# Gelu of an MLP taken one token tile at a time, between the exponentials of an attention that shares ScalarE with it

## The chip, the cores and the metric

The kernel runs on one core of one Trainium2 chip. The metric is the device time of one execution in microseconds (us), here the median of the runs. The core has five engines that each work through their own list of instructions in order: TensorE (PE in the profile, with PEld for the loading of weights), VectorE (DVE), ScalarE (ACT), GpSimd (POOL) and SyncE (SP), which here only issues DMAs. They wait for each other by semaphores.

## The reference

Two layers of the same kind follow each other on 2048 tokens of width 512. Each has an attention part with 32 query heads of width 16 that share one key and one value head, and a part B with a token-shifting mixer and an MLP. Cut to what matters:

```python
def _A_ref(x, wq, wk, wv, wo):              # S = 2048, D = 512, H = 32, Dh = 16
    q = (x @ wq).reshape(B, S, H, Dh).transpose(0, 2, 1, 3)
    k, v = x @ wk, x @ wv                   # one head for all queries
    p = _softmax(jnp.einsum("bhqd,bkd->bhqk", q, k) * (Dh ** -0.5))
    return jnp.einsum("bhqk,bkd->bhqd", p, v)....reshape(B, S, H * Dh) @ wo

def _B_ref(x, w1, w2, w3, w4):              # F = 1792
    h = _gelu(_layernorm(x) @ w1)           # tanh form of gelu
    ...                                     # the four quarters of h are shifted by +1, -1, +2, -2 tokens
    x1 = x + shifted @ w2
    return x1 + _gelu(_layernorm(x1) @ w3) @ w4

x = x + _A_ref(_layernorm(x), ...)
x = x + _B_ref(_layernorm(x), ...)          # and both once more, with the same weights
```

## The kernel before

The program is laid out by a list scheduler that runs while the kernel is built. Every operation is declared with the tags that it reads and writes, an estimated duration `dur` and a priority (a lower number goes first); the scheduler walks through an estimated time, gives each engine the ready operation with the lowest number, and so fixes the order of each engine's instructions and the semaphores between them. On the chip only that order and those waits remain: where the estimate was too early, an engine stands still; where it was too late, work is placed later than it could be.

Tokens come in 16 tiles of 128, grouped in chunks. Layer 0 has four chunks of four tiles; layer 1 has three of four and two of two tiles:

```python
CHUNKS = (((0, 4), (4, 4), (8, 4), (12, 4)),
          ((0, 4), (4, 4), (8, 4), (12, 2), (14, 2)))
EARLY = (6, 11)      # layer 1, chunk 0: key tiles 0-5 first, then 6-10, then 11-15
SPILLED = 7          # for so many blocks of four heads; their sums are spilled in between
```

The attention of a chunk is cut into blocks of four heads, and these into halves: two heads, 512 queries and 128 keys (two key tiles and 256 queries in short chunks), that is 128x1024 scores. The whole program has 2048 halves. A half goes one of two ways. As a *unit*, ScalarE takes the exponential of both heads at once from PSUM:

```python
def declare_unit(self, g):
    ...
    q = op("PE", fpe, reads=self.inputs(g), writes=bk, ...)            # scores = K^T Q into PSUM
    o = op("ACT", lambda e: e.activation(self.EA[:, ea, :, :], self.PB[:, b0:b0 + 2, :], ACTF.Exp, scale=0.25),
           writes=bk + [("EA", ea)], dur=0.06 + 1024 / 1200, prio=0, ...)
    self.add_pv(g, ...)                                                # times V, summed in the PSUM bank ACC
```

As a *pair*, VectorE and GpSimd take it: VectorE scales the scores to 16-bit integers that are read as bf16 (J), one instruction per head; GpSimd, or VectorE if GpSimd has a queue, makes two shifted copies (JK); and the three are multiplied with three scaled copies of V, which averages the error of the piecewise-linear exponential:

```python
def assign(self, now, p):                    # may the next half be a pair?
    ...                                      # x pairs at most may be unfinished
    if self.pl.backlog() > y or self.waiting and ...:
        return False
    ...
    self.declare_pair(g)
```

When a block's sum is complete, VectorE copies it out of ACC, which frees ACC for the next block; ACCF, RZ and OS, the buffers of the steps that follow, are each two deep:

```python
def block_end(self, la, c, b, end):
    m = self.nfin % 2
    acc, rz = self.ACCF[:, m, 0:n], self.RZ[:, m, 0:4 * nq]            # n = 512, or 256 in short chunks
    self.last_copy = op("DVE", lambda e: e.tensor_copy(acc, self.PB[:, self.ACC, 0:n]), writes=[("AC",), ("ACCF", m)], ...)
    ...                                      # row sums, reciprocal, spread by TensorE
    op("DVE", ... self.OS[:, m, 0:n] = acc * spread ..., reads=[("ACCF", m)], writes=[M, ("OS", m)])
    ...                                      # OS goes to OT by DMA, or by TensorE in the last blocks
```

When all eight blocks of a chunk are done, `chunk_end` declares its output projection, mixer and MLP, which run beside the attention of later chunks. The MLP lags by one tile, because the mixer needs tokens of the next chunk: it runs for tiles 0-2, 3-6, 7-10 and, in layer 0, 11-13 and 14-15.

```python
def chunk_end(self, la, c):
    ...
    if m < 0:
        self.qproj(la, c + 2, prio=11)       # Q of the chunk after next, staged in QS and moved to QT by DMA
    self.mixer_in(la, c, tiles, tail, ...)
    ...
    for p in ([grp] if len(grp) <= 4 else [grp[:3], grp[3:]]):
        self.mlp(la, p, tail, self.DEFER[la][c])
    self.next_kv(la, c)                      # layer 0: K and V of layer 1 for the finished tiles

def mixer_in(...):
    ...                                      # x W1 on TensorE, copied to GP by VectorE
    op("ACT", fg, reads=gt + ..., writes=gt + ..., dur=2.7 + 4 * n / 1200 + ..., prio=-1)   # gelu of GP in place

def mlp(self, la, tiles, tail, defer=False):
    ...                                      # layer norm, transposes
    for f in range(14):
        ...                                  # 128 of the 1792 features: W3 on TensorE (128x32 pieces, four side by side)
        op("DVE", ... self.G2[:, f, 0:n] <- PSUM ..., writes=[L, ("G2", f)])
    g2 = [("G2", f) for f in range(14)]
    def fgelu(e):
        for a in (0, 7):                     # two instructions, seven feature blocks of all tiles each
            ins = e.activation(self.G2[:, a:a + 7, 0:n], self.G2[:, a:a + 7, 0:n], ACTF.Gelu_apprx_tanh)
        return ins
    if not tail:
        op("ACT", fgelu, reads=g2, writes=g2, dur=2.8 + 14 * n / 1200, prio=-1)
    self.mlp_out(la, tiles, tail)            # per tile: 56 products with W4, then the residual added by VectorE
```

The exponential and the gelu need different activation tables, so that the program holds a table load ahead of each change from one to the other. Where TensorE would have nothing to do for long, the scheduler puts in filler products of zeros (`ONES,NIL`), which keep it active.

Of the kernel before, what the change touches and what calls it, by code (L numbers as in the profile page):

```python
# [26 lines left out]
class Op:  # L27
    __slots__ = ("eng", "emit", "preds", "npend", "succ", "dur", "prio", "seq", "ready", "start",
                 "end", "take", "give", "dma", "out", "pos", "sem", "vc", "side", "placed", "pe", "feeds", "port", "parts")


class Plan:
# [65 lines left out]
    def op(self, eng, emit, reads=(), writes=(), dur=0.1, prio=None, take=None, give=None,  # L98
           dma=0, out=False, side=True, pe=None, port=False, parts=1):
# [5 lines left out]
        o.parts = parts  # L105
        o.feeds = None
# [204 lines left out]

    def backlog(self):
        return sum(o.dur for o in self.heap["DVE"] if o.side and o.ready <= self.now + 0.5)

    def _place(self, o, t):
# [31 lines left out]
        else:  # L347
# [5 lines left out]
            o.end = t + wait + o.dur + self.DRAIN[o.eng]  # L353
# [152 lines left out]
class Kernel:  # L506
# [20 lines left out]
    DEFER = ((False, False, False, False, False), (False, False, False, False, False))  # L527
# [11 lines left out]
    SOON = 0.45  # L539

# [23 lines left out]
    def memory(self):  # L564
# [24 lines left out]
        self.OS = sb("OS", [2, 512])  # L589
# [11 lines left out]
        self.ACCF = sb("ACCF", [2, 512])  # L601
        self.RZ = sb("RZ", [2, 16])
# [57 lines left out]
    def head(self):  # L660
# [70 lines left out]
        self.qproj(0, 1)  # L731
# [72 lines left out]
    def ln_in(self, la, tiles, prio=None):  # L804
# [6 lines left out]
        base = (self.QS, "QS") if la else (self.ZR, "ZR")  # L811
# [54 lines left out]
    def qproj(self, la, c, prio=None, blocks=range(8), direct=False):  # L866
        op = self.pl.op
        tiles = self.tiles_of(la, c)
# [5 lines left out]
        for k in () if direct else range(blocks[0] // 2, blocks[-1] // 2 + 1):  # L874
            L = Late()
            for h in range(2):
# [7 lines left out]
            op("DVE", lambda e, k=k, L=L: e.tensor_copy(self.QS[:, k, 0:n], self.PB[:, L.bank, 0:n]),  # L884
               writes=[L, ("QS", k)], dur=t_ps(n), prio=prio, give=L)
        if not direct:
            k0, k1 = blocks[0] // 2, blocks[-1] // 2 + 1
            for j in range(2):
                op("SP", lambda e, j=j: [
                    e.dma_start(self.QT[32 * h:32 * h + 16, par, 2 * k0 + j:2 * k1:2, 0:n],  # L890
                                self.QS[64 * j + 16 * h:64 * j + 16 * h + 16, k0:k1, 0:n]) for h in range(4)],
                   reads=[("QS", k) for k in range(k0, k1)], writes=[("QT", par, 2 * k + j) for k in range(k0, k1)],
# [20 lines left out]
    def make_groups(self):  # L913
# [49 lines left out]
        self.later = None  # L963
# [141 lines left out]
    def block_end(self, la, c, b, end):  # L1105
# [12 lines left out]
        m = self.nfin % 2  # L1118
        self.nfin += 1
        n = self.size(la, c)  # L1120
        nq = n // 128
        acc, rz = self.ACCF[:, m, 0:n], self.RZ[:, m, 0:4 * nq]
        if end == "add":
# [3 lines left out]
               reads=tags, writes=[("AC",), ("ACCF", m)], dur=t_ps(512), prio=0, side=False)  # L1127
        else:
            self.last_copy = op("DVE", lambda e: e.tensor_copy(acc, self.PB[:, self.ACC, 0:n]),  # L1129
               writes=[("AC",), ("ACCF", m)], dur=t_ps(n), prio=0, side=False)  # L1130
# [9 lines left out]
        op("PE", fz, reads=[("ACCF", m), ("SELC",)], writes=[L], pe=("F", 60 * nq, 4 * nq), prio=fin, take=L)  # L1140
# [4 lines left out]
        op("DVE", frec, writes=[L, ("RZ", m)], dur=0.17, prio=fin, give=L)  # L1145
        M = Late()
        for h in range(nq // 2):
# [8 lines left out]
            op("PE", fx, reads=[("RZ", m), ("ID",)], writes=[M], pe=("P", 256, 256, range(4)), prio=fin,  # L1156
               take=M if h == 0 else None)
        op("DVE", lambda e: e.tensor_tensor(out=self.OS[:, m, 0:n], in0=acc, in1=self.PB[:, M.bank, 0:n],  # L1158
                                            op=ALU.mult),
           reads=[("ACCF", m)], writes=[M, ("OS", m)], dur=t_ps(n), prio=fin, give=M)  # L1160
        r0 = 64 * (b % 2)
        hw = n // 2
        if c == len(self.CHUNKS[la]) - 1 and b >= self.LATE_OT:
            N = Late()

            def fo(e):
                ins = None
                for u in range(2):
                    for p in range(2):
                        x = r0 + 32 * p  # L1170
                        ins = e.matmul(self.PB[x:x + 32, N.bank, u * hw:u * hw + hw], lhsT=self.SELO[:, u, :],
                                       rhs=self.OS[:, m, p * hw:p * hw + hw], start=True, stop=True,
                                       tile_position=(0, x), skip_group_check=True)
                return ins
            op("PE", fo, reads=[("OS", m)] + [("SELO", i, u) for i in range(2) for u in range(2)], writes=[N],
# [3 lines left out]
        else:  # L1179
            op("SP", lambda e: [  # L1180
                e.dma_start(self.OT[r0 + 16 * (2 * p + i):r0 + 16 * (2 * p + i) + 16, b // 2, u * hw:u * hw + hw],
                            self.OS[32 * (2 * i + u):32 * (2 * i + u) + 16, m, p * hw:p * hw + hw])
                for p in range(2) for i in range(2) for u in range(2)],
               reads=[("OS", m)], writes=[("OT", b)], dma=128 * n, parts=8, prio=fin)
# [40 lines left out]
    def assign(self, now, p):  # L1225
# [8 lines left out]
        if sum(1 for o in self.pairs[-4:] if not (o.placed and o.end <= now + 1e-9)) >= x:  # L1234
            return False
        if self.pl.backlog() > y or \
# [18 lines left out]
    def chunk_end(self, la, c):  # L1255
# [9 lines left out]
        if m < 0:  # L1265
            self.qproj(la, c + 2, prio=11)
        later, self.later = self.later, None
        self.mixer_in(la, c, tiles, tail, later and later[0])
        if later:
            later[1]()  # L1270
# [231 lines left out]
```

## Time and profile before

The median of three runs is 1595.02 us (1594.45 to 1596.03). The profiled execution had a span of 1596.4 us, at a mean granted TensorE clock of 0.997.

| ScalarE work in the program | instructions | busy us |
|---|---|---|
| exponentials of units, 128x1024 | 1489 | 1382.5 |
| gelu of the MLP (four, three or two tiles, in two instructions each) | 18 | 46.0 |
| gelu of the mixer, 128x2048 and 128x1024 | 8 | 14.5 |
| gelu straight from PSUM in the last tiles | 18 | 7.4 |
| table loads | 30 | 38.5 |

Of the 2048 halves 1489 are units and 559 are pairs; the latter show as 1118 J instructions on VectorE.

The page gives, in order, the busy time and its share for each engine, the busy share in 40 equal slices, the DMA queues, the chain of waits that ended last, the costliest groups of instructions (a group is a line of the kernel with an engine, an operation and a shape; behind the bar stand its busy time, the mean duration of one, and the idle time of the engine just before the group with what ended it) and the DMA issues. Instructions of one engine can overlap by a little, so that the busy time of a group is less than its count times the mean of one. The instruction order of the built program, which needs no run, tells in addition after how many exponentials each gelu stands and what lies between two products on TensorE.

### The profile page before, as it was taken

To read this page: it belongs to the slowest core of one execution; us is meant where nothing else is said; L and a number is where in the kernel's file an instruction comes from. 1 tells how busy PE (TensorE), PEld (TensorE's weight loads), DVE (VectorE), ACT (ScalarE), POOL (GpSimd) and SP (SyncE) were. 2 spreads that over 40 slices of the span, in tenths; PEclk is the share of its full clock that TensorE was granted. 3 is DMA by queue.
4 is the path that set the end of the run, shared out by engine and by line. 5 is a ranking of instruction groups with operands and counts; after the bars stand their busy time and mean duration, and the time that the engine had idled before them with its cause. 6 is when DMAs were issued, how large, how long until landed. Compare 5 with 4: busy or idle time off the path is not lost.

```text
span 1596.4 us, 63539 instructions
## 1 busy us (share of the span) xinstructions
PE 1553.2 (97%) x28725; PEld 659.9 (41%) x28725; DVE 1272.6 (80%) x2258; ACT 1488.7 (93%) x1563; POOL 1101.5 (69%) x1116
## 2 busy tenths in 40 slices
PE   8999999999999999999999999999999999999999
PEld 3333343343333333334344334434343344545545
DVE  8888887887888879888876688888687886778863
ACT  4999999999999999999958899999999999988972
POOL 4788777877676676787724577786777877577641
PEclk9999999999999999999999999999999999999999
DMA  6100010000000000100000000100000000000000
GB/s 210 17 6 6 6 19 4 7 4 4 14 11 6 5 4 6 20 3 2 2 3 2 2 8 11 19 4 6 14 12 8 4 4 13 19 8 5 8 10 26
DMA packets 32144, 21.54 MB, mean 13 GB/s; under 512 B 12672, under 2 KB 31360, under 8 KB 31872
## 3 DMA queue, kind: packets, MB, share of 16 engines
q1 hardware_dynamic: 31872, 17.47, 4.6%
q8 instruction: 224, 3.67, 1.0%
q14 instruction: 48, 0.39, 0.1%
HBM read 7.90 MB, written 2.10 MB: 6 GB/s over the span
## 4 chain that ended last, share of the span: by engine, by line
PE 49%; ACT 43%; DVE 6%; issue 1%; POOL 1%; DMA 0%; SPq 0%
ACT EA L1018 39%; PE PB L974 16%; PE PB L626 16%; PE PB L1097 14%; DVE J L1039 2%; ACT G L1429 2%; PE PB L792 1%; ACT L1018 1%; DVE ST L737 1%; ACT GP L1349 1%; DVE G L1422 1%; PE PB L902 0%; POOL JK L1049 0%; PE PB L1152 0%; PE PB L1137 0%
## 5 line engine op out<-in xcount | busy, mean ns | idle before, releaser
L1018 ACT ACTIVATE EA<-PB 128x1024 bf16<-128x1024 f32 x1489 | 1382.5, 1068 | 46.7 <-PE PB L974 29.5
L1049 POOL TENSOR_SCALAR JK<-J 128x1024 uint16<-128x1024 uint16 x922 | 977.9, 1061 | 389.3 <-DVE J L1039 236.6
L1039 DVE TENSOR_SCALAR J<-PB 128x512 uint16<-128x512 f32 x1118 | 722.5, 682 | 158.0 <-PE PB L974 153.4
L974 PE MATMUL PB<-QT,KT 32*128 32x512 bf16 (+1 forms) x4608 | 635.1, 360 | 24.1 <-ACT EA L1018 13.3
L1097 PE MATMUL PB<-EA,VP 128*32 128x256 bf16 (+1 forms) x6716 | 378.4, 264 | 2.3 <-DVE ACCF L1129 1.2
L974 PEld LDWEIGHTS PB<-QT,KT 32*128 32x128 bf16 x4608 | 164.7, 91 | 423.9 <-ACT EA L1018 285.0
L1097 PE MATMUL PB<-JK,VD 128*32 128x256 bf16 (+1 forms) x5000 | 298.6, 266 | 1.5 <-POOL JK L1049 1.2
L1097 PEld LDWEIGHTS PB<-EA,VP 128*32 128x32 bf16 x6716 | 158.9, 95 | 148.6 <-issue 118.3
L1097 PEld LDWEIGHTS PB<-JK,VD 128*32 128x32 bf16 x5000 | 118.5, 95 | 138.2 <-issue 89.7
L626 PE MATMUL PB<-ZT,W 128*32 128x512 bf16 (+2 forms) x2816 | 167.3, 342 | 0.5 <-DVE J L1039 0.4
L1097 PE MATMUL PB<-J,VD 128*32 128x256 bf16 (+1 forms) x2500 | 160.1, 266 | 1.4 <-DVE J L1039 1.0
L626 PE MATMUL PB<-ONES,NIL 128*32 128x512 bf16 x1620 | 143.3, 392 | 7.1 <-DVE ZR L774 1.8
L1049 DVE TENSOR_SCALAR JK<-J 128x1024 uint16<-128x1024 uint16 x196 | 131.3, 677 | 12.4 <-PE PB L1097 11.1
L626 PE MATMUL PB<-W,G 128*32 128x512 bf16 x1624 | 115.3, 383 | 0.1
L1422 DVE CAST G<-PB 128x512 bf16<-128x512 f32 (+2 forms) x126 | 71.8, 580 | 17.6 <-PE PB L626 16.5
L1097 PEld LDWEIGHTS PB<-J,VD 128*32 128x32 bf16 x2500 | 62.0, 96 | 46.1 <-issue 30.9
L626 PEld LDWEIGHTS PB<-ZT,W 128*32 128x32 bf16 x2816 | 66.6, 96 | 29.1 <-issue 13.3
L1429 ACT ACTIVATE G<-G 128x3584 bf16<-128x3584 bf16 (+2 forms) x18 | 46.0, 2600 | 31.7 <-DVE G L1422 31.6
L626 PEld LDWEIGHTS PB<-ONES,NIL 128*32 128x32 bf16 x1620 | 40.0, 97 | 43.8 <-issue 10.6
L1158 DVE TENSOR_TENSOR OS<-ACCF,PB 128x512 bf16<-128x512 bf16 (+1 forms) x72 | 44.6, 621 | 12.2 <-PE PB L1152 11.7
L757 POOL TENSOR_TENSOR SM<-SM,MH 128x4 f32<-128x4 f32 (+3 forms) x39 | 36.5, 935 | 21.0 <-DVE SM L759 18.3
L626 PEld LDWEIGHTS PB<-W,G 128*32 128x32 bf16 x1624 | 37.0, 96 | 27.6 <-issue 13.6
(94 smaller groups left out, 863.7 us busy)
## 6 DMA issues: line engine op xcount, KB each, us to landing
OT<-OS SPq DMA_DIRECT2D x424, 8.0 KB, 1.7
W<-in_B_w_dram SPq DMA_DIRECT2D x2, 1792.0 KB, 14.5
QT<-QS SPq DMA_DIRECT2D x40, 64.0 KB, 2.4
X<-in_A_x_dram SPq DMA_DIRECT2D x8, 256.0 KB, 5.5
out_dram<-OUTB SPq DMA_DIRECT2D x16, 128.0 KB, 1.8
OT<-OS SPq DMA_DIRECT2D x104, 4.0 KB, 1.8
W<-in_B_w_dram SPq DMA_DIRECT2D x2, 512.0 KB, 8.6
WQ<-in_A_wq_dram SPq DMA_DIRECT2D x1, 512.0 KB, 4.3
```

The costliest lines, as they stand in the source:

```text
L626: ins = e.matmul(self.PB[32 * g:32 * g + 32, bank, 0:n], lhsT=lhsT[:, 32 * g:32 * g + 32], rhs=rhs, start=start, stop=stop, tile_position= ...
L737: op("DVE", lambda e, tb=tb: e.bn_stats(self.ST6[:, tb, :], src(tb)), reads=[tagf(tb)], writes=[("ST", tb)], dur=0.606, prio=prio)
L757: op("POOL", lambda e: e.tensor_tensor(out=out, in0=src, in1=self.MH[:, 0, a:b], op=ALU.pow), reads=tags + [("MH",)], writes=tg(r), dur=0. ...
L792: ins = e.transpose(self.PBH[:, L.bank, j * 512 + i * 128:j * 512 + (i + 1) * 128], rows[:, tb % 4, dc * 128:(dc + 1) * 128], self.IDENT)
L974: ins = e.matmul(self.PB[:, bank, j * n:(j + 1) * n], lhsT=self.KT[32 * h:32 * h + 32, la, (kb + j) * 128:(kb + j + 1) * 128], rhs=self.QT ...
L1018: o = q.feeds = op("ACT", lambda e: e.activation(self.EA[:, ea, :, :], self.PB[:, b0:b0 + 2, :], ACTF.Exp, scale=0.25), writes=bk + [("EA" ...
L1039: o = op("DVE", lambda e, i=i, L=L: e.tensor_scalar(out=J[:, i * 512:(i + 1) * 512], in0=self.PB[:, L.bank, :], scalar1=128 * LOG2E * 0.25 ...
L1049: x = op(eng, lambda e, k=k, r=r: e.tensor_scalar(out=self.JK[:, r, :], in0=J, scalar1=float(self.STEPS[k]), scalar2=1.0, op0=ALU.add, op1 ...
L1097: ins = e.matmul(self.PB[32 * x:32 * x + 32, self.ACC, p * hw:p * hw + hw], lhsT=v[:, la, kb + j, :], rhs=ap[:, i, j * w + u * hw:j * w + ...
L1158: op("DVE", lambda e: e.tensor_tensor(out=self.OS[:, m, 0:n], in0=acc, in1=self.PB[:, M.bank, 0:n], op=ALU.mult), reads=[("ACCF", m)], wri ...
L1422: op("DVE", lambda e, f=f, L=L: e.tensor_copy(self.G2[:, f, 0:n], self.PB[:, L.bank, 0:n]), writes=[L, ("G2", f)], dur=t_ps(n), give=L)
L1429: ins = e.activation(self.G2[:, a:a + 7, 0:n], self.G2[:, a:a + 7, 0:n], ACTF.Gelu_apprx_tanh)
```

## The change

It does four things.

1. The gelu of the MLP is one instruction per token tile, over all 14 feature blocks, where it was two instructions of seven blocks for all tiles. The W4 products of a tile then wait for that tile's gelu alone. New tags (`GE`, f, i) carry this. The scheduler's estimate for a gelu now tells the table load ahead of it from the one behind it: `after` is the part of `dur` that the engine is taken for, but that its consumers don't wait for.
2. ACCF, RZ and OS are cut into four parts for short chunks (256 columns) and stay two for long ones.
3. No further pair is assigned while VectorE has over 0.7 us of urgent work in its queue (`queue`, `QUEUE`).
4. Q of layer 0's chunks 2 and 3 is computed with that of chunk 1 at the start, staged in G2 (chunk 2) and QS (chunk 3), and at the chunk ends only moved. The normalised rows of layer 1's first tiles are therefore put in ZR and not QS.

The unused `DEFER` path goes. The core of the diff:

```diff
+    def queue(self):
+        return self.free_at["DVE"] - self.now + sum(o.dur for o in self.heap["DVE"] if o.prio <= 2)
...
-            o.end = t + wait + o.dur + self.DRAIN[o.eng]
+            o.end = t + wait + o.dur - o.after + self.DRAIN[o.eng]
...
+    QUEUE = 0.7
...
-        self.qproj(0, 1)
+        for c in (1, 2, 3):
+            self.qproj(0, c, part="make" if c > 1 else None)
...
-        base = (self.QS, "QS") if la else (self.ZR, "ZR")
+        base = (self.QS, "QS") if la and tiles[0] > 2 else (self.ZR, "ZR")
...
-        m = self.nfin % 2
+        m = self.nfin % (1024 // n)
+        parts = range(2 * m, 2 * m + 2) if n == 512 else (m,)
+        am, zm, om = ([(x, i) for i in parts] for x in ("ACCF", "RZ", "OS"))
...
+        if self.pl.queue() > self.QUEUE:
+            return False
         if self.pl.backlog() > y or \
...
-            self.qproj(la, c + 2, prio=11)
+            self.qproj(la, c + 2, prio=11, part=None if la else "move")
...
-            op("ACT", fg, reads=gt + (more[0] if more else []), writes=gt + (more[0] if more else []),
-               dur=2.7 + 4 * n / 1200 + (more[2] if more else 0), prio=-1)
+            op("ACT", lambda e: e.activation(self.GP[:, par, :, 2:2 + n], self.GP[:, par, :, 2:2 + n],
+                                             ACTF.Gelu_apprx_tanh),
+               reads=gt, writes=gt, dur=2.94 + 4 * n / 1200, prio=-1, after=1.4)
...
-        g2 = [("G2", f) for f in range(14)]
-        def fgelu(e):
-            ins = None
-            for a in (0, 7):
-                ins = e.activation(self.G2[:, a:a + 7, 0:n], self.G2[:, a:a + 7, 0:n], ACTF.Gelu_apprx_tanh)
-            return ins
...
-        if not tail:
-            op("ACT", fgelu, reads=g2, writes=g2, dur=2.8 + 14 * n / 1200, prio=-1)
+        for i in range(len(tiles)) if not tail else ():
+            ends = (i == 0) + (i == len(tiles) - 1)
+            op("ACT", lambda e, i=i: e.activation(self.G2[:, :, i * 128:(i + 1) * 128], self.G2[:, :, i * 128:(i + 1) * 128],
+                                                  ACTF.Gelu_apprx_tanh),
+               reads=[("G2", f, x) for f in range(14) for x in range(4)], writes=[("GE", f, i) for f in range(14)],
+               dur=0.107 + 1792 / 1200 + 1.35 * ends, prio=-1, after=1.35 if i == len(tiles) - 1 else 0.0)
         self.mlp_out(la, tiles, tail)
```

In the instruction order of the built program the counts move like this:

| | before | after |
|---|---|---|
| exponentials of units on ScalarE | 1489 | 1499 |
| table loads on ScalarE | 30 | 32 |
| gelu of the MLP on ScalarE | 18 (up to 128x3584) | 29 (128x1792 each) |
| J on VectorE (two per pair) | 1118 | 1098 |
| JK on VectorE / GpSimd | 196 / 922 | 173 / 925 |
| filler products on TensorE | 1620 | 1552 |

## The prediction

> **What bounds the kernel now.** I read the totals of the page first, then the costliest groups.
>
> ```profile
> PE 1553.2 (97%) x28725; PEld 659.9 (41%) x28725; DVE 1272.6 (80%) x2258; ACT 1488.7 (93%) x1563; POOL 1101.5 (69%) x1116
> ...
> L1018 ACT ACTIVATE EA<-PB 128x1024 bf16<-128x1024 f32 x1489 | 1382.5, 1068 | 46.7 <-PE PB L974 29.5
> ...
> L626 PE MATMUL PB<-ONES,NIL 128*32 128x512 bf16 x1620 | 143.3, 392 | 7.1 <-DVE ZR L774 1.8
> ```
>
> TensorE is called busy for 97%, but 143.3 us of that are fillers, so it has slack. ScalarE has 1488.7 us of work that nothing can shorten on the spot, and 1596.4 - 1488.7 = 107.7 us of idle time. So the time is ScalarE's work plus its gaps, and I ask where the gaps are. The busy times by stretch, with cuts that I chose where the 40 slices show ScalarE below 9 (columns: window; its length, then busy time of PE, PEld, DVE, ACT, POOL; clock; DMA):
>
> ```profile
> 0.00:19.50 19.50, 15.05 (x201) 5.85 (x205) 15.85 (x42) 1.29 (x2) 13.22 (x23) 1.00 0.94 301
> 19.50:43.00 23.50, 23.44 (x380) 10.52 (x374) 21.18 (x54) 20.01 (x22) 5.18 (x6) 1.00 0.37 106
> 43.00:780.00 737.00, 720.38 (x12202) 286.35 (x12202) 615.58 (x1047) 734.86 (x780) 562.10 (x556) 1.00 0.04 8
> 780.00:925.00 145.00, 140.03 (x2474) 61.72 (x2466) 99.26 (x198) 115.22 (x111) 68.97 (x73) 0.99 0.01 2
> 925.00:1400.00 475.00, 466.95 (x8722) 195.12 (x8716) 387.23 (x664) 473.89 (x499) 347.98 (x342) 1.00 0.05 10
> 1400.00:1460.00 60.00, 56.03 (x1472) 29.02 (x1470) 46.73 (x88) 49.17 (x51) 45.20 (x51) 0.94 0.04 7
> 1460.00:1536.25 76.25, 75.34 (x2084) 38.92 (x2077) 63.75 (x120) 76.06 (x81) 49.14 (x54) 1.00 0.03 6
> 1536.25:1596.40 60.15, 56.03 (x1222) 32.37 (x1222) 23.07 (x51) 18.19 (x23) 9.74 (x15) 1.00 0.07 22
> ```
>
> Length minus ACT gives the gaps: head 18.2 + 3.5, layer 0's middle 2.1, the passage from layer 0 to layer 1 29.8, then 1.1, the short chunks 10.8, then 0.2, and the tail 42.0. Sum 107.7. The two long middles have no gap to win: there only the amount of ScalarE's work counts. ScalarE's timeline in the passage:
>
> ```profile
> 787.05 1.91 ACT L1349 ACTIVATE GP<-GP 128x2048 bf16<-128x2048 bf16 x1
> 788.87 6.26 ACT L1429 ACTIVATE G<-G 128x3584 bf16<-128x3584 bf16 x2
> ...
> 811.47 1.28 ACT L1429 ACT_TABLE_LOAD   x1
> 830.39 4.78 ACT L1429 ACTIVATE G<-G 128x2688 bf16<-128x2688 bf16 x2 [17.64 <-DVE G L1422]
> ...
> 861.82 8.51 ACT L1018 ACTIVATE EA<-PB 128x1024 bf16<-128x1024 f32 x9 [5.24 <-PE PB L1097]
> ```
>
> The gelu of tiles 7-10 (128x3584) comes only at 788.87, right behind the mixer gelu of the last chunk. K and V of layer 1 for those tiles hang on it, so after 14 more exponentials ScalarE has nothing but the next gelu, and that waits 17.64 us for VectorE's copies, which wait for a TensorE that is doing the W4 products of tiles 7-10 and the W3 products of tiles 11-13 at once. The releaser named, VectorE, isn't the cause; the late gelu is.
>
> **What the skill says.** The Trainium skill, "ScalarE: Activation LUTs", section "What ACT_TABLE_LOAD costs", gives about 1283 ns for a load plus a drain of about 1380 ns, so 2.66 us a switch. The trace agrees on the load (1283 ns) and shows no such drain: the exponentials end at 804.48 + 6.97 = 811.45 and the load starts at 811.47. I take 1.28. The same section has one element per cycle at 0.833 ns and 186 ns fixed, with neighbours overlapping by about 93 ns, so an estimate of 1.59 us for each further gelu of 1792 elements; the trace has 1689 ns for one and 3.29 us for two, so 1.60 for each further one. It agrees. "Perfetto Trace Analysis", section "Identifying the Most-Contended Engine", warns that TensorE's busy share is no measure of how near it is to its limit; the fillers above agree.
>
> **The change, part by part.** Only the order and the counts of the built program are used for what the chip will do.
>
> Work on ScalarE: ten more exponentials. In the stretch from 925 to 1400 the group is busy 448.75 us for 485 (the same windows asked for that tile alone), 0.925 each: +9.3 us. Two more table loads, since the gelu of tiles 7-10 no longer stands beside the mixer's: +2.6. The gelu of the MLP: nine runs (four of four tiles, three of three, two of two) cost 46.0 before (the group's busy time); after, a run of four tiles takes 1.69 + 3 x 1.60 = 6.49, of three 4.89, of two 3.29, and 26.0 + 14.7 + 6.6 = 47.2: +1.2. Together +13.1, all on the path.
>
> The passage: with Q of chunks 2 and 3 made early, the chain of chunk 2 runs ahead. The gelu of tiles 7-10 now stands after exponential 718 (790 before), the last mixer gelu after 793 (790), the gelu of tiles 11-13 after 837 (804), that of 14-15 after 867 (835). So 44 and 30 exponentials lie in the two intervals where there were 14 and 31, and K of tiles 6-10 is long there. 29 more at 0.925 are 26.8 us of work that fills the 24.9 us of gaps between 787 and 873 (1.27 + 17.64 + 5.24 + 0.72); the 17.64 us wait and the 5.24 us one should go. What stays is read from the order on TensorE: between the score products of exponentials 882 and 883 stand the transposes of tiles 12-15, their K and V products and 32 fillers. Before, that chain took from the last normalised row (end 901.74) to the copy of K (end 908.03) 6.3 us; two exponentials wait in their banks, so 6.3 - 1.85 = 4.4 us of idle time. In two more places (before 807 and 857) some 3.4 us of matmuls (counted at the rates of the timeline) stand between two score products, where 1.85 are covered: 1.5 each. Sum 7.4; I take 9 for what the order doesn't show. 29.8 to 9: -20.8.
>
> The short chunks: the largest gap is this one.
>
> ```profile
> 1404.65 0.41 DVE L1158 TENSOR_TENSOR OS<-ACCF,PB 128x256 bf16<-128x256 bf16 x1
> ...
> 1405.43 0.41 DVE L1129 CAST ACCF<-PB 128x256 bf16<-128x256 f32 x1
> ...
> 1406.25 2.85 ACT L1018 ACTIVATE EA<-PB 128x1024 bf16<-128x1024 f32 x3 [5.57 <-PE PB L1097]
> ```
>
> The copy out of ACC needs a free ACCF, and that one is freed by the multiplication in front of it, which had itself stood behind a normalisation. No PV product could run, so no exponential's buffer came free: 5.57 us. Four buffers take that wait away. The other 5.1 us come after the mixer gelu at 1433, where 64 mixer products run in one piece (3.88 us) and at a lower clock (0.91). After the change 32 stand there, and beside the gelu. I leave 1.5 of 10.8: -9.3.
>
> The tail: TensorE-bound from the last exponential, 56.0 busy of 60.15. The same products stand there, but 32 of the first tiles' W4 products move ahead of the output projection, where fillers were, since they need one tile's gelu (1.28 + 1.69 us after the last exponential) and not four tiles' (7.5). 104 such products took 5.79 us: 32 are 1.8; I take -1.5.
>
> The W4 products of the middle now start inside the gelu run, in bursts of 88 to 128 (4.9 to 7.1 us at that rate), in a time in which ScalarE needs no scores: the run with its loads lasts 1.28 + 6.49 + 1.28 = 9.05. They cost nothing, and gain nothing, for the middles had no gaps. The head is the same: 0. The rule on pairs acts through the counts above.
>
> Sum: +13.1 - 20.8 - 9.3 - 1.5 = -18.5. Span 1596.4 - 18.5 = 1577.9; the median of before lies 1.4 under its span, so **1576.5**.
>
> **The rivals.** (1) The gelu bursts starve the scores: if TensorE is late by 1 to 2 us after each of the eight runs that have exponentials behind them, as it was after the 64 mixer products (2.6), 8 to 16 us are lost, and the time is 1585 to 1593. For it: the largest burst alone fills 7.1 of 9.05 us, and PV products stand beside it. Against it: scores for two exponentials lie ready when a run begins. (2) The passage moves its wait instead of losing it: only 13 exponentials stand between the last gelu (867) and the first that needs tile 11's K (880); the chain from that gelu to K took 31.4 us before (876.68 to 908.03). If it stays so long, 31.4 less about 15 exponentials and a load (15.2) leaves 16.2 instead of 4.4: some 1588. Against it: W4 for two tiles is 112 products, 6 us, and the rest was drawn out by work put between. (3) The ten extra exponentials cost nothing, because they fall into gaps that I count as staying: 1576.5 - 9.3 = 1567. For it: the passage has 29 more of them, so the stretches without gaps have fewer. Against it: I have already counted those 29 as filling the passage's gaps, and can't count them twice.
>
> **Range and chances.** The work (+13) is sure within 1 us; the passage may give 12 to 26, the short chunks 5 to 10, bursts may take up to 10. That gives **1568 to 1589** for 8 in 10. Faster by over 2% (under 1563.1) needs all gaps but head and tail to vanish: 0.05. Slower by over 2% needs a stall that nothing in the order shows: 0.02. Within 2%: 0.93.
>
> **What would show it.** Right: ScalarE's busy time near 1502; its idle time in the passage near 9 with no wait of a gelu on VectorE over 3 us; no gap of 5 us in the short chunks; a tail of 58 to 59 us after the last exponential. Wrong: gaps behind each gelu run that TensorE ends (rival 1), a gap over 10 us just before tile 12's scores (rival 2), or exponentials at another pace than 0.925.

## The result, and the profile after

The changed kernel takes 1573.22 us in the median (1572.56 to 1574.09, four runs) against 1595.53 of the kernel before: a ratio of 0.985 with a 95% interval of 0.9818 to 0.9882. The predicted time was 1576.5. The profiled execution of before took 1598.2 us, 3.2 more than the median that the prediction started from, and that of the changed kernel 1574.1; so the spans of the two profiles differ by 24.1 us and the medians by 22.3. The totals and two groups of the page of the changed kernel, the counterparts of those shown of before:

```profile
PE 1538.2 (98%) x28569; PEld 655.3 (42%) x28569; DVE 1252.4 (80%) x2215; ACT 1497.2 (95%) x1586; POOL 1105.6 (70%) x1119
...
L1027 ACT ACTIVATE EA<-PB 128x1024 bf16<-128x1024 f32 x1499 | 1387.2, 1086 | 35.0 <-PE PB L983 26.9
```

ScalarE's busy time rose by 8.5 us (1488.7 to 1497.2) and its idle time fell from 107.7 to 1572.3 - 1497.2 = 75.1. The stretches that changed, with the cuts moved to the same places of the program (columns as in the prediction: window; length, then busy PE, PEld, DVE, ACT, POOL; clock; DMA):

```profile
790.00:935.00 145.00, 141.47 (x2487) 59.58 (x2476) 101.61 (x188) 133.43 (x137) 83.68 (x84) 1.00 0.01 3
...
1410.00:1470.00 60.00, 58.92 (x1638) 30.88 (x1630) 50.83 (x101) 59.77 (x64) 45.66 (x50) 1.00 0.03 7
...
1515.10:1572.30 57.20, 53.74 (x1182) 35.34 (x1182) 22.46 (x51) 18.46 (x26) 8.69 (x14) 1.00 0.07 23
```

Length less ACT: the passage between the layers has 11.6 us of idle time where it had 29.8, the short chunks 0.2 where they had 10.8, the tail 38.7 where it had 42.0. ScalarE's timeline in the passage (start, length, instruction, and in brackets the idle time ahead of it with what ended it):

```profile
798.64 1.91 ACT L1355 ACTIVATE GP<-GP 128x2048 bf16<-128x2048 bf16 x1
...
815.18 30.71 ACT L1027 ACTIVATE EA<-PB 128x1024 bf16<-128x1024 f32 x33 [3.13 <-PE PB L1106]
...
847.20 4.87 ACT L1433 ACTIVATE G<-G 128x1792 bf16<-128x1792 bf16 x3
...
872.57 12.24 ACT L1027 ACTIVATE EA<-PB 128x1024 bf16<-128x1024 f32 x13 [3.16 <-PE PB L1106]
...
909.56 21.19 ACT L1027 ACTIVATE EA<-PB 128x1024 bf16<-128x1024 f32 x23 [4.99 <-PE PB L983]
```

In the passage no gelu waits for VectorE any more. Three gaps stay, before exponentials 805, 855 and 883; the prediction had named 807, 857 and 883.

To compare runs below, I cut each profiled execution in the same way: the gaps of ScalarE in the passage (from 765 to 925 us) and in the short chunks (from 1375), everything else up to the last exponential (the head of 21 to 24 us is in it), and the tail from there. A gap is an idle time of over 0.15 us. "Work" is the time up to the last exponential without its gaps. Each row adds up to its span but for roundings.

| kernel | exponentials | work | passage | short chunks | other gaps | tail | span |
|---|---|---|---|---|---|---|---|
| before | 1489 | 1473.4 | 29.4 | 10.6 | 22.8 | 60.2 | 1596.4 |
| changed | 1499 | 1481.2 | 11.3 | 0 | 22.6 | 57.2 | 1572.3 |
| before + early Q | 1492 | 1474.5 | 24.0 | 3.8 | 26.4 | 65.0 | 1593.8 |
| before + one-tile gelu | 1484 | 1469.9 | 18.1 | 1.4 | 24.4 | 61.0 | 1574.8 |
| before + pair rule | 1498 | 1480.6 | 13.0 | 5.8 | 25.2 | 65.7 | 1590.5 |
| before + split buffers | 1488 | 1467.6 | 29.2 | 0.3 | 24.7 | 73.7 | 1595.6 |
| changed - pair rule | 1492 | 1477.1 | 8.8 | 3.6 | 26.5 | 57.5 | 1573.4 |
| changed - split buffers | 1497 | 1479.7 | 11.3 | 1.5 | 21.4 | 57.2 | 1571.1 |
| changed - early Q | 1499 | 1480.2 | 10.2 | 0 | 22.1 | 57.2 | 1569.7 |
| changed - one-tile gelu | 1498 | 1488.0 | 12.6 | 1.5 | 23.0 | 54.6 | 1579.7 |
| before + estimates | 1490 | 1472.0 | 15.7 | 3.0 | 34.2 | 59.9 | 1584.9 |
| before + one-tile gelu, joint wait | 1486 | 1473.1 | 11.1 | 5.4 | 35.7 | 63.0 | 1588.3 |
| changed, one estimate 1 ns less | 1494 | 1476.8 | 6.2 | 0 | 22.9 | 57.6 | 1563.4 |
| before, one estimate 1 ns less | 1492 | 1477.4 | 21.7 | 12.5 | 36.2 | 65.2 | 1613.0 |

These are single profiled executions; the times that count are the medians given with each experiment. One kernel takes longer where an execution's granted clock is lower (the kernel before 1594.8 us at 0.999 and 1603.3 at 0.991), and the profiled execution of the joint wait, at 0.991, took 8.5 us more than its median.

### The profile page after: what moved, and what is told of

It is laid out like the page before. It is cut to its first block, busy times and chain, and to the rows that moved or that the text cites. A ratio compares the mean times of both kernels' runs of the same rounds, so it can differ in the third digit from the quotient of the medians.

```text
span 1572.3 us, 63149 instructions
## 1 busy us (share of the span) xinstructions
PE 1538.2 (98%) x28569; PEld 655.3 (42%) x28569; DVE 1252.4 (80%) x2215; ACT 1497.2 (95%) x1586; POOL 1105.6 (70%) x1119
## 4 chain that ended last, share of the span: by engine, by line
ACT 64%; PE 33%; DVE 2%; DMA 0%; issue 0%; POOL 0%; SPq 0%; DVEq 0%; POOLq 0%
ACT EA L1027 59%; PE PB L983 11%; PE PB L630 10%; PE PB L1106 9%; ACT G L1433 2%; ACT L1027 1%; PE PB L797 1%; ACT GP L1355 1%; DVE J L1048 1%; ACT L1433 0%; ACT L1355 0%; DMA X<-in_A_x_dram 0%; PE PB L840 0%; PE PB L1163 0%; PE PB L1148 0%; DVE JK L1058 0%
## 5 line engine op out<-in xcount | busy, mean ns | idle before, releaser
L1027 ACT ACTIVATE EA<-PB 128x1024 bf16<-128x1024 f32 x1499 | 1387.2, 1086 | 35.0 <-PE PB L983 26.9
L1048 DVE TENSOR_SCALAR J<-PB 128x512 uint16<-128x512 f32 x1098 | 711.4, 682 | 141.6 <-PE PB L983 136.9
L983 PE MATMUL PB<-QT,KT 32*128 32x512 bf16 (+1 forms) x4608 | 626.4, 360 | 19.5 <-ACT EA L1027 9.5
L1106 PE MATMUL PB<-EA,VP 128*32 128x256 bf16 (+1 forms) x6760 | 388.9, 265 | 1.9 <-DVE ACCF L1140 0.9
L1106 PE MATMUL PB<-JK,VD 128*32 128x256 bf16 (+1 forms) x4912 | 291.6, 266 | 1.9 <-POOL JK L1058 0.8
L630 PE MATMUL PB<-ZT,W 128*32 128x512 bf16 (+2 forms) x2816 | 171.8, 342 | 0.1
L1058 DVE TENSOR_SCALAR JK<-J 128x1024 uint16<-128x1024 uint16 x173 | 114.8, 669 | 9.0 <-PE PB L1106 7.4
L630 PE MATMUL PB<-W,G 128*32 128x512 bf16 x1624 | 104.2, 380 | 1.1 <-ACT G L1433 1.1
L1433 ACT ACTIVATE G<-G 128x1792 bf16<-128x1792 bf16 x29 | 47.0, 1686 | 12.6 <-DVE G L1428 12.5
L630 PEld LDWEIGHTS PB<-W,G 128*32 128x32 bf16 x1624 | 42.6, 96 | 33.5 <-issue 8.1
L762 POOL TENSOR_TENSOR SM<-SM,MH 128x4 f32<-128x4 f32 (+3 forms) x39 | 37.4, 959 | 21.6 <-DVE SM L764 18.8
```

The costliest lines, as they stand in the source:

```text
L630: ins = e.matmul(self.PB[32 * g:32 * g + 32, bank, 0:n], lhsT=lhsT[:, 32 * g:32 * g + 32], rhs=rhs, start=start, stop=stop, tile_position= ...
L762: op("POOL", lambda e: e.tensor_tensor(out=out, in0=src, in1=self.MH[:, 0, a:b], op=ALU.pow), reads=tags + [("MH",)], writes=tg(r), dur=0. ...
L983: ins = e.matmul(self.PB[:, bank, j * n:(j + 1) * n], lhsT=self.KT[32 * h:32 * h + 32, la, (kb + j) * 128:(kb + j + 1) * 128], rhs=self.QT ...
L1027: o = q.feeds = op("ACT", lambda e: e.activation(self.EA[:, ea, :, :], self.PB[:, b0:b0 + 2, :], ACTF.Exp, scale=0.25), writes=bk + [("EA" ...
L1048: o = op("DVE", lambda e, i=i, L=L: e.tensor_scalar(out=J[:, i * 512:(i + 1) * 512], in0=self.PB[:, L.bank, :], scalar1=128 * LOG2E * 0.25 ...
L1058: x = op(eng, lambda e, k=k, r=r: e.tensor_scalar(out=self.JK[:, r, :], in0=J, scalar1=float(self.STEPS[k]), scalar2=1.0, op0=ALU.add, op1 ...
```

## The experiments

The theory on record has four claims about which part of the change does what: early Q brings the gelu of tiles 7-10 forward and so empties the passage; four-deep buffers remove the 5.57 us gap; the pair rule acts only through the counts; the one-tile gelu gives 1.5 us in the tail and otherwise nothing. The rival to all four is that any reordering which lets chunk 2's MLP finish in time does the same.

### One part alone on the kernel before

**Early Q.**

```diff
-        self.qproj(0, 1)
+        for c in (1, 2, 3):
+            self.qproj(0, c, part="make" if c > 1 else None)
...
-            self.qproj(la, c + 2, prio=11)
+            self.qproj(la, c + 2, prio=11, part=None if la else "move")
...
```

> The kernel before with early Q alone. The prediction's theory (early Q is what brings the gelu of tiles 7-10 forward, and with it the passage's 21 us): the passage loses most of its 30 us of gaps, about 1575. Rival (early Q has nothing to do with it; it needs a faster way from mixer gelu to MLP gelu): in the instruction order the gelu of tiles 7-10 still stands right behind the last mixer gelu, after exponential 787, so the 17 us wait stays; three exponentials more (+2.8), the two gaps of the short chunks gone (-8), the tail 3 us longer: about 1593.

Measured: 1593.91 us, ratio 0.9984 (0.9976 to 0.9992). The timeline of ScalarE in the passage:

```profile
788.46 6.26 ACT L1435 ACTIVATE G<-G 128x3584 bf16<-128x3584 bf16 x2
...
832.75 4.78 ACT L1435 ACTIVATE G<-G 128x2688 bf16<-128x2688 bf16 x2 [16.68 <-DVE G L1428]
```

The gelu of tiles 7-10 still starts behind the last mixer gelu, at 788.46 (788.87 before), and the next one waits 16.68 us for VectorE (17.64 before). The theory's first claim falls.

**One-tile gelu**, with its new estimates for both gelus.

```diff
-            for a in (0, 7):
-                ins = e.activation(self.G2[:, a:a + 7, 0:n], ...)
+        for i in range(len(tiles)) if not tail else ():
+            op("ACT", ... self.G2[:, :, i * 128:(i + 1) * 128] ..., writes=[("GE", f, i) for f in range(14)], ..., after=...)
```

> The kernel before with one-tile gelu and its new estimates alone. The prediction's theory: the passage keeps its gaps, only the tail gains 1.5 us and the two more table loads cost 2.6: about 1596. Rival (the one-tile gelu itself brings the chain forward): in the order the gelu of tiles 7-10 stands after exponential 738 and there are only 1484 exponentials, 15 fewer than in the changed kernel: 1573.2 - 13.9 + 3.6 for a longer tail + 3 for gaps behind the gelu of tiles 14-15, about 1566.

Measured: 1576.75 us, ratio 0.9874 (0.9851 to 0.9896). This part alone brings 18.8 of the 22.3 us. Between the profiled executions, which lie 21.6 us apart, it comes from work 3.5 (five exponentials fewer), passage 11.3, short chunks 9.2, against 1.6 more in other gaps and 0.8 in the tail. The rival's order was right and its size too large: gelus still wait for VectorE twice in the passage, as here.

```profile
828.30 4.87 ACT L1430 ACTIVATE G<-G 128x1792 bf16<-128x1792 bf16 x3 [4.46 <-DVE G L1425]
...
854.14 3.28 ACT L1430 ACTIVATE G<-G 128x1792 bf16<-128x1792 bf16 x2 [5.73 <-DVE G L1425]
```

**Pair rule.**

```diff
+        if self.pl.queue() > self.QUEUE:
+            return False
```

> The kernel before with the rule on VectorE's queue alone. The prediction's theory: the rule only moves halves from pairs to units; nine exponentials more (+8.3) and no gap less, about 1603. Rival (any reordering that lets chunk 2's MLP finish before chunk 3's attention ends empties the passage): the gelu of tiles 7-10 stands after exponential 747, the passage gains about 20, the short-chunk gap of 5.6 stays, the tail is 5 us longer: about 1579.

Measured: 1593.05 us, ratio 0.9982 (0.9974 to 0.999). Both sides are half right: the passage empties to 13.0, but nine more exponentials (work +7.2) and a longer tail (+5.5) take most of it back.

**Split buffers.**

```diff
-        m = self.nfin % 2
+        m = self.nfin % (1024 // n)
+        parts = range(2 * m, 2 * m + 2) if n == 512 else (m,)
...
```

> The kernel before with ACCF, RZ and OS split for short chunks alone. Up to exponential 1367 the order of ScalarE is that of the kernel before. The prediction's theory: the 5.6 us gap goes and perhaps the other 5 too, 1585 to 1590. Rival (the order that follows loses more than the gap): the last mixer gelu but one moves from after exponential 1461 to after 1488, the last one, and TensorE has 67.6 us of columns left after the last score product instead of 53.7: minus 5.6, minus 2.6 for two loads fewer, plus 13.9, about 1600.

Measured: 1595.46 us, ratio 0.9992 (0.9982 to 1.0002), no difference. The gap did go: the short chunks have 0.3 us of gaps where they had 10.6. It came back in the tail, which grew from 60.2 to 73.7. The timeline there:

```profile
1523.24 1.06 ACT L1351 ACTIVATE GP<-GP 128x1024 bf16<-128x1024 bf16 x1
1535.18 6.27 ACT L1431 ACTIVATE G<-G 128x3584 bf16<-128x3584 bf16 x2 [10.88 <-DVE G L1424]
```

The attention finished earlier, but the chain of chunk 2's mixer and MLP was no further, so the gelu of tiles 7-10 waits 10.88 us for its input where before it waited for none. A gap removed from ScalarE ahead of a chain that sets the end is no time won.

### The changed kernel with one part undone

**Without the pair rule.**

```diff
-        if self.pl.queue() > self.QUEUE:
-            return False
```

> The changed kernel without the rule on VectorE's queue. Theory 1 (the rule keeps ScalarE fed, and its ten extra exponentials are the price): without it gaps come back, about 1580. Theory 2 (the rule only costs here, since the gaps are gone by the other parts): seven exponentials fewer (-6.5), gaps of the order 2.7 instead of 5.6 (-2.9): about 1564.

Measured: 1577.46 us, ratio to the kernel before 0.989 (0.9873 to 0.9906). That is 4.2 us more than the changed kernel, though seven exponentials fewer stand on ScalarE: the work falls by 4.1, and gaps of one to two us come back in several places (other gaps +3.9, short chunks +3.6). The time lies nearer to theory 1; counting exponentials and the large holes in the order missed these gaps. Part of the 4.2 us goes with the granted clock: two executions at 0.999 and 1.0 took 1576.0 and 1575.3 us, two at 0.996 and 0.997 took 1579.7 and 1578.9.

**Without split buffers.**

```diff
-        m = self.nfin % (1024 // n)
+        m = self.nfin % 2
...
```

> The changed kernel with ACCF, RZ and OS two deep in short chunks too. The prediction's theory (four buffers remove the 5.57 us gap): the gap comes back, about 1578. Rival (the gap was one collision of the order before and is gone with the new order anyway): the order is the changed kernel's nearly to the end, no gap of that kind in it, two exponentials fewer: about 1571.5.

Measured: 1573.82 us, ratio 0.9864 (0.985 to 0.9879): as the changed kernel. The gap isn't there with two buffers either; the only one left in that stretch is this.

```profile
1448.25 21.43 ACT L1027 ACTIVATE EA<-PB 128x1024 bf16<-128x1024 f32 x23 [1.30 <-PE PB L1106]
```

The claim that four buffers remove the 5.57 us falls for the change as a whole. Two buffers alone don't make that gap; it also took an order like that of the kernel before.

**Without early Q.**

```diff
-        for c in (1, 2, 3):
-            self.qproj(0, c, part="make" if c > 1 else None)
+        self.qproj(0, 1)
...
```

> The changed kernel with Q of chunks 2 and 3 made at the chunk ends again. The prediction's theory (early Q brings the gelu of tiles 7-10 forward): about 1593. Rival: that gelu stands after exponential 727, the passage stays almost free of gaps, 1499 exponentials as in the changed kernel: 1571 to 1573.

Measured: 1572.29 us, ratio 0.9854 (0.984 to 0.9869). Nothing is lost without it: passage 10.2.

**Without one-tile gelu.** The estimates stay those of the changed kernel to within 0.23 us; only the instruction is cut the old way and the W4 products wait for it all.

```diff
-        for i in range(len(tiles)) if not tail else ():
-            op("ACT", ... self.G2[:, :, i * 128:(i + 1) * 128] ..., writes=[("GE", f, i) ...], ...)
+        op("ACT", fgelu, reads=..., writes=[("GE", f, x) for f in range(14) for x in range(4)],
+           dur=0.2 + 14 * n / 1200 + 2.7, prio=-1, after=1.35)
```

> The changed kernel with the MLP's gelu in two instructions of seven blocks again, the W4 products waiting for all of it; estimates, early Q, rule and buffers stay. If the one-tile gelu is what empties the passage: about 1593. If it gives only its 1.5 us in the tail: one exponential fewer (-0.9), two loads more (+2.6), the gelu 1.2 shorter, gaps of the order much alike, the tail 2.8 shorter because tiles 7-10 are done before the last exponential: about 1571.

Measured: 1582.62 us, ratio 0.9917 (0.9902 to 0.9931): 9.4 us more than the changed kernel, between the two expectations. The passage stays short (12.6): the gelu of tiles 7-10 still stands well ahead of the last mixer gelu, after exponential 744 and not 777. The pair rule and the new estimates are still in, and each alone moved that gelu forward in the kernel before (to 747 and 773 from 790); which of them does it here isn't shown. Most of the loss sits in the work up to the last exponential (+6.8), of which two more table loads and a gelu of tiles 7-10 that now stands before the last exponentials are the known part.

### Pieces, estimates, or the order itself

**The new estimates alone.**

```diff
-               dur=2.7 + 4 * n / 1200 + (more[2] if more else 0), prio=-1)
+               dur=2.94 + 4 * n / 1200 + (more[2] if more else 0), prio=-1, after=1.4)
...
-            op("ACT", fgelu, reads=g2, writes=g2, dur=2.8 + 14 * n / 1200, prio=-1)
+            op("ACT", fgelu, reads=g2, writes=g2, dur=2.9 + 14 * n / 1200, prio=-1, after=1.35)
...
```

> The kernel before with the new estimates alone: for its two-instruction gelu and for the mixer's, the table load behind a gelu no longer counts for those who wait for it. Theory P (the pieces matter: W4 products that start inside the gelu run bring the next chain forward): the W4 products of tiles 3-6 still take 46 exponentials from first to last (50 before, 17 changed), the last mixer gelu but two stays at exponential 670 (672 before), so most of the gain is missing: 1585 to 1593. Theory E (the estimates matter): the 5.6 us gap is gone from the order and the passage is shorter: 1576 to 1582.

Measured: 1585.56 us, ratio 0.9929 (0.9913 to 0.9945), at the lower edge of theory P. The passage falls to 15.7, and 10.6 us of new gaps appear in layer 1's middle, where there were none.

**One-tile gelu and estimates, but all W4 products of a run wait for all of its tiles.**

```diff
-            g2 = [("EA", f // 2) if tail else ("GE", f, i) for f in range(14)]
+            g2 = [[("EA", f // 2)] if tail else [("GE", f, x) for x in range(4)] for f in range(14)]
```

> As the run of one-tile gelu and estimates alone (1576.75), but every W4 product waits for the gelu of all tiles of its run; so the gelu stays in one-tile instructions, and the early start of the W4 products is taken away. Theory P: 1585 to 1593. Theory E: as with the early start, 1575 to 1579. In the order, the gelu of tiles 7-10 stands after exponential 742, before the last mixer gelu (773), as in the kernels with a short passage.

Measured: 1581.68 us, ratio 0.9913 (0.9892 to 0.9934): 4.9 us more than with the early start, between both theories. The passage is short (11.1) without it. Where the 4.9 us are lost isn't shown: of the 9.9 us of gaps that the profile has in layer 0's middle, 4.8 lie between 440 and 455, where the granted clock was 0.54.

**One estimate in the changed kernel 1 ns smaller.** It is the time that the scheduler adds between two operations on the same engine.

```diff
-    SELF = 0.035
+    SELF = 0.034
```

> The changed kernel with one number of the scheduler's estimates one nanosecond smaller (SELF 0.034 for 0.035): the same operations, rules and buffers, but another order: 1494 exponentials instead of 1499, and in the passage one place of 2.0 us that isn't covered where there were three. If the time is set by the four parts of the change: 1573. If it is set as much by which order the scheduler happens on: five exponentials (-4.6) and about 4 us of gaps less, about 1564.

Measured: 1565.06 us (1564.39 to 1565.28), ratio 0.9801 (0.9782 to 0.9819). The rules and buffers are those of the changed kernel; only the order differs, and with it five halves that are pairs and not units. It is 8.2 us faster; it is the fastest kernel of this study. Its passage has 6.2 us of gaps, the largest this one.

```profile
863.72 7.54 ACT L1027 ACTIVATE EA<-PB 128x1024 bf16<-128x1024 f32 x8 [3.45 <-PE PB L1106]
...
879.39 41.73 ACT L1027 ACTIVATE EA<-PB 128x1024 bf16<-128x1024 f32 x45 [0.28 <-PE PB L983]
```

The 4.99 us before tile 12's scores is gone.

**One estimate in the kernel before 1 ns smaller.** It is the time for a change between kinds of products on TensorE.

```diff
-    SWITCH = 0.097
+    SWITCH = 0.096
```

> The kernel before with one number of the scheduler's estimates one nanosecond smaller (SWITCH 0.096 for 0.097): the same operations and rules in another order. If the order that the scheduler happens on matters little: 1595. If it matters: three exponentials more (+2.8), places between scores that aren't covered of 14.7 us instead of 7.3, 4.6 us more on TensorE after the last scores, and the passage of the kind before: about 1605.

Measured: 1611.12 us, ratio 1.0089 (1.007 to 1.0109), slower than the kernel before by more than the expectation had. Its six executions had a granted clock of 0.992 to 0.996, and the time fell from 1614.9 to 1609.1 us over that range; continued to 0.999, where the kernel before takes 1595, that gives about 1605 (an estimate). By that, some 10 of the 15.4 us go with the order and the rest with the clock. Whether this order is what lowers the clock isn't shown. The buffer gap of the short chunks is here the longest of all:

```profile
1419.38 12.40 ACT L1018 ACTIVATE EA<-PB 128x1024 bf16<-128x1024 f32 x13 [7.87 <-PE PB L1097]
```

## Why the prediction was right, and which of its steps were wrong

The time was predicted within 3.3 us. The sum was taken from the order of the changed program itself, and its main terms, a passage and short chunks with few gaps left, came true. That it came so close is in part luck: orders that were priced in the same way above were met within 1.1 us with early Q alone and with SELF changed, but the chip was 6 to 14 us slower than priced with the one-tile gelu alone (1566), the pair rule alone (1579), two-instruction gelu put back (1571), the rule taken out (1564) and SWITCH changed (1605). The terms, beside the table's rows for before and changed:

| term | predicted | measured |
|---|---|---|
| ScalarE's work | +13.1 | +7.8 |
| passage | -20.8 | -18.1 |
| short chunks | -9.3 | -10.6 |
| tail | -1.5 | -3.0 |
| head and other gaps | 0 | -0.2 |
| sum of the span | -18.5 | -24.1 |

The span came out 5.6 us lower than predicted, and the step from a span to a median made up for 2.3 of them: the prediction took 1.4 us off, because the profile of before lay so much over its median, and in the changed kernel the median lies 0.9 above the span.

**Work.** The mis-sized term (ScalarE's busy time as a whole, with the tail, rose by 8.5). Table loads (+2.6) and gelu (46.0 to 47.0) came as worked out. Ten more exponentials were put at 9.3 us; the group's busy time rose by 4.7 (1382.5 to 1387.2), so one exponential fell from 0.9285 to 0.9254 us on the mean. The step multiplied a count by the pace of an undisturbed stretch and forgot that those that were already there ran slower in the disturbed ones. In the traces an exponential that starts while the one before it still runs adds 0.92 us, and one that starts on an idle engine 1.02. Of the latter there were 76 before and 57 after, 38 and 30 of them behind idle times too short to show as a gap in the timeline: 19 x 0.10 = 1.9 us of the missing 4.6. The other 2.7 are a pace of the former that is 2 ns faster each; what held them up before stays open.

**Passage.** The three places read from the order on TensorE were the three gaps: 4.4 predicted and 4.99 measured before tile 12's scores, 1.5 twice predicted and 3.13 and 3.16 measured. The two latter were too small because ScalarE there waits for PV products, which give the buffers of the exponentials back; I had counted only the scores. In both places a block ends, and its last PV products stand behind the piece of work that I had counted. VectorE then copies the sum out of ACC, and the trace has the PV products of the next block let go by that copy. For the gap of 3.13:

```profile
814.09 0.69 DVE L1124 COPY QT<-PB 128x512 f32<-128x512 f32 x1
...
814.83 0.56 PEld L1106 LDWEIGHTS PB<-EA,VP 128*32 128x32 bf16 x24 [0.58 <-DVE QT L1124]
...
815.18 1.02 ACT L1027 ACTIVATE EA<-PB 128x1024 bf16<-128x1024 f32 x1 [3.13 <-PE PB L1106]
```

QT holds a spilled sum here. The 24 products let go at once belong to six exponentials: none of the new block's PV products could run before the copy. It is the wait for ACC that the short chunks had, but a copy into the spilled sum needs no ACCF, so that splitting ACCF leaves it as it is.

The passage as a whole was right in size and wrong in its cause: the step that said "with Q of chunks 2 and 3 made early, the chain of chunk 2 runs ahead" is false. Early Q alone leaves the gelu where it was (24.0 us of gaps), and the change without it has a passage of 10.2. The order of the program shows that the gelu came forward; it doesn't show which edit did it, and I took the edit that touched Q.

**What did bring it forward.** The kernels with the gelu of tiles 7-10 right behind the last mixer gelu have the long passages: before, early Q and split buffers, with 24.0 to 29.4, then the kernel before with one estimate 1 ns less (21.7) and the estimates alone (15.7). Those with it well ahead have 6.2 to 18.1. One-tile gelu with its estimates and the pair rule each sufficed in the order that they made. For the one-tile gelu the prediction had said of the W4 bursts that "they cost nothing, and gain nothing, for the middles had no gaps". They cost nothing: no gelu run in the middles has a gap of even 1 us behind it. They may also gain, which I had ruled out. In the order, the W4 products of tiles 3-6 before stood spread over 50 exponentials; in the changed kernel over 17, because most are done while ScalarE is at the gelu. TensorE's timeline at that run in the changed kernel, and ScalarE's beside it:

```profile
531.53 7.09 PE L630 MATMUL PB<-W,G 128*32 128x512 bf16 x128 [0.17 <-ACT G L1433]
```

```profile
529.78 6.46 ACT L1433 ACTIVATE G<-G 128x1792 bf16<-128x1792 bf16 x4
536.26 1.28 ACT L1027 ACT_TABLE_LOAD   x1
```

128 of the products (groups of four by 32 columns) lie in one stretch from 531.53 to 538.62. It is let go by the first of the four gelus, which ends one quarter into the 6.46 us, and so lies under the three others and the table load but for its last 1.1 us. In the kernel before, the products waited for the whole gelu and began at 562.21, when the exponentials, and with them the scores, begin too (562.36).

That this start is what brings the next chain forward is argued and not shown. The mixer gelu of chunk 2 comes after exponential 632 in the changed kernel and 672 before, and the gelu of tiles 7-10 86 exponentials behind it and not 118. But without the early start (joint wait) the mixer gelu stands after 643, and the passage is short; with the pair rule alone the W4 products stay spread over 50 exponentials, and it stands after 649. So a short passage doesn't need early W4 products. What the runs do show is that an order can put the gelu of tiles 7-10 up to 72 exponentials earlier by changes in a stretch without gaps, and that the gaps taken away by it lie some 100 us later; the prediction valued each stretch by its own gaps alone. How much of the 18.8 us belongs to the early W4 products and how much to the new estimates is not settled: estimates alone 10.1, both without the early start 14.0, and differences of that size also come from 1 ns.

**Short chunks.** The wait for ACCF was read rightly in the kernel before, and split buffers do remove it there. In the changed kernel it is absent with two buffers as well, so the part of the gain that was put down to them isn't theirs. The other 5.1 us of the kernel before stand where its profiled execution had a granted clock of 0.77 (1433 to 1447; the prediction's 0.91 is the mean of a longer stretch). So part of the 10.6 may go with that clock and not with the order.

**Tail.** Right in its mechanism: in the changed kernel 32 of the first tile's W4 products begin at 1518.17, ahead of the output projection at 1519.90. The tail fell by 3.0 where 1.5 had been taken.

**Pair rule.** "Acts through the counts above" was wrong: without it there are seven exponentials fewer and 4.2 us more. In the changed kernel's order it keeps small gaps of ScalarE away, at the price of more exponentials; alone on the kernel before it left more of the other gaps (25.2 for 22.8) and gained 2.5 us.

**Rivals.** The gelu bursts starve no scores (rival 1). The passage kept a wait before tile 12, but of 4.99 us and not 16.2 (rival 2). Rival 3, that the extra exponentials fall into gaps that stay, named the direction of the error (the work rose by 7.8 and not 13.1), though not its cause.

**What stays open.** The four parts alone give -1.6, -18.8, -2.5 and -0.1, each against the before beside it, and the sum is near the whole by chance: undone from the changed kernel they give -0.9, +9.4, +4.2 and +0.6. A change of 1 ns in an estimate gave -8.2 and +15.4. Two such changes don't give a spread, but a part's effect of some 10 us or less in one order can't be told from the effect of having another order. Only the one-tile gelu put in with its estimates (18.8) lies above both; taken out with the estimates left in it gave 9.4, which does not. What the other three parts are worth in another order isn't shown.

## What to carry to other kernels

Where a scheduler lays out the program, price the order it made, not the edit: the count of the bound engine's instructions and the holes between its inputs gave the time to 0.2% here and to 0.9% at worst in the runs above, while the story of which edit caused it was wrong in three of four cases, and in the fourth (the buffers) held only in the kernel before. Before crediting an edit with less than about 1%, change an estimate by a hair and see how far the time moves by itself; then keep the best of several such orders. And a gap removed on the busiest engine is won only if the chain that ends the program moves with it.

## What the runs showed of the hardware

Change of function on ScalarE cost one table load of 1283 ns in every kernel here, with nothing visible ahead of it: in the changed kernel the exponentials ahead of the gelu above end at 528.47 and the load starts at 528.49. A gelu of 1792 elements as 14 rows of 128 costs what one of 7 rows of 256 did: 1686 ns on the mean against 1689. An exponential of 128x1024 from PSUM took 1.02 us alone and added 0.92 us behind a running one (means of 1024 and 922 ns in the changed kernel). The time went with the granted clock: 1594.8 us at 0.999 and 1603.3 at 0.991 for the kernel before, 1.1 us for each 0.001.
